# Clustered attention ahead of two expert stages: four re-ordered steps in the attention's slot schedule

## The chip, the cores and the metric

One core of one Trainium2 chip runs the whole program in one launch. The metric is the device time of the launch in microseconds (us), the median over the runs. Engines are named as the profile names them: PE is TensorE's matmul, PEld its weight load, DVE is VectorE, ACT is ScalarE, POOL is GpSimd, SP is SyncE, which here only issues DMAs. A "q" behind an engine's name is its instruction queue.

## The reference

Attention in which a query sees only keys of its own cluster, then two feed-forward stages. Shapes: 2 batches, 8 heads, 768 positions, head size 64, 16 clusters; the feed-forward stages see 1536 tokens of width 512.

```python
q_assign = argmax(normalised(q) @ normalised(centroids).T)      # per head, 16 clusters
k_assign = argmax(normalised(k) @ normalised(centroids).T)
scores = where(q_assign[:, None] == k_assign[None, :], q @ k.T / 8, -1e9)
attn = softmax(scores)                                          # over 768 keys
x = (attn @ v).reshape(1536, 512)
x = (silu(x @ w_gate) * (x @ w_val)) @ w_out                    # 512 -> 1536 -> 512
out = sum_e p[:, e] * (relu(x @ w1[e]) @ w2[e])                 # 4 experts, 512 -> 1024 -> 512
```

All of it is in 32-bit floats. The kernel gets near that precision out of faster matmuls by splitting operands in a high and a low part ("hi" and "lo", `xh` and `xl`, `wuh` and `wul`), so a product is two or three matmuls.

## The kernel before

`attention()` runs first, then `moe()`. The order of all instructions is written by hand; each engine takes its own in program order and waits for semaphores.

The attention works on 16 heads `g` (2 batches of 8), each in two halves of 384 queries, which makes 32 units `u`, and each unit in three parts, which makes 96 slots (`slot = 3u + t`). A pair `p` of heads takes 12 slots, a head 6, a unit 3. In every slot the letters of `ORDER = "ESTLAtVMlvZB"` are run through (line 564):

- `S`: four matmuls of the scores of a row block that is 5 slots ahead (`s_mm`, L325 and L326), into one of two pairs of PSUM banks;
- `M`: VectorE's row minimum or maximum over those 768 scores (`s_max`, L331); `E`: ScalarE's exponential of the block before (`s_exp`, L342), which frees the scores' bank;
- `T` and `t`: three transposes each of the exponentials (`transp`, L348), with ScalarE's copy `hi` out of PSUM (L353);
- `l` and `L`: VectorE's `lo = ps - hi` (`low`, L367), `l` for the first of the slot's two key blocks, `L`, one slot later, for the second. For the last key block of a unit `low` is a plain copy `pT` (L361);
- `V` and `v`: the products with v for the two key blocks of the slot before (`pv`, L378, L383, L384), accumulated over a unit into the tile `pv`, of which there is one PSUM bank only (`bufs=1`, line 185). So the first product of a unit (`V` in the slot with t = 1) cannot start before the bank of the unit before has been copied out;
- `A`, `Z`, `B`: extra tasks hung on a slot by `at(slot, pos, fn)` and `steps(base, when, generator)`; `("-13a", "2z")` means the generator's next step 13 slots before base at `A`, then 2 slots after it at `Z`.

The copy out of the bank is `pv_out` (lines 386 to 407). It is called at `v` in the slot with t = 0 right behind the unit's last product (`v_step`, line 587). For the pairs 0 to 6 (28 units) it is one ScalarE copy (L395), for the last pair a ScalarE copy and a VectorE add (L406, L407). Behind the fourth unit of a pair three SP DMAs move halves of `x` between partitions (L400 to L402).

The extra tasks that the change touches:

- `recip(p)` (line 409): VectorE sums and inverts the row sums of a pair, PE transposes them (L416), ScalarE copies them out, SP writes them to DRAM (`rd`, L421) and in the same step issues two DMAs (L424) that read them back, spread over 64 partitions each, as `R`. SP waits at L424 until `rd` has landed. `norm(p, G)` uses `R` at slot 9 of the pair behind, on GpSimd.
- `cluster(g)` (line 244): 12 matmuls against the centroids (L259), then the choice of the cluster. From g = 3 on it runs GpSimd `sc - mx` (L282), ScalarE `sc * HUGE` (L284), GpSimd `sc + wtie` (L286), VectorE's maximum (L288), GpSimd's subtraction (L290), ScalarE's step function (L292), 6 transposes (L296), and ScalarE writes the mask rows `mk` (L305), which two SP DMAs bring into the head's operand `t` (`t<-mk`, L307). The 12 matmuls stand 13 slots ahead of a head, the mask's DMAs 9 slots ahead; the first score matmul of that head stands 5 slots ahead of it.
- `w_steps` (line 103): the first chunk of feed-forward weights comes as 64-bit floats and is converted in 4 pieces of 512 columns. A piece is 5 steps: two ScalarE conversions with VectorE's sign mask (L113, L114, L115) and the SP load of a later piece (`w_load`, L89); VectorE's clamp (L118); shift and or (L120); add (L122); ScalarE's high part with VectorE's low part (L125, L126). Lines 556 to 561 hang these on slots 0 to 7 of every pair from p = 1 on.
- `load_v(g)` (line 229): two SP DMAs and a GpSimd DMA, 8 slots ahead of a head; `rest_v` on GpSimd (L240) 4 slots ahead. `load_qk` and `rest_qk` (L219, L220, L226) load a head's q and k on GpSimd's queue and compute their low parts on GpSimd.

`moe()` begins when the last unit is out: its matmuls (L164, L761, L858, L891) follow each other on PE with no slot schedule.

Of the kernel before, what the change touches and what calls it, by code (L numbers as in the profile page):

```python
# [7 lines left out]
F32 = mybir.dt.float32  # L8
# [4 lines left out]
ACTF = mybir.ActivationFunctionType  # L13
# [23 lines left out]
def tile_cluster_attention_moe(ctx, tc, qk, vt, cent, consts, wm1, wm2, probs, out):  # L37
# [64 lines left out]

    def w_steps(k, part, o):

        if k[0] == 1:
# [6 lines left out]
            ai = a.bitcast(I32)  # L112
            A.activation(out=a, in_=w1.bitcast(F32), func=ACTF.Abs, scale=2.0 ** -112)  # L113
            A.activation(out=ri, in_=w0.bitcast(U32), func=ACTF.Copy, scale=2.0 ** -29)  # L114
            V.tensor_scalar(out=mi, in0=w1, scalar1=-2**31, scalar2=None, op0=ALU.bitwise_and)  # L115
# [8 lines left out]
            wh, wl = w_tile(k, part, o)  # L124
            A.copy(out=wh[:, s], in_=a)  # L125
            V.tensor_tensor(out=wl[:, s], in0=a, in1=wh[:, s].bitcast(F32), op=ALU.subtract)  # L126
            yield
# [47 lines left out]
    def attention():  # L175
        with ExitStack() as ax:
# [67 lines left out]
            def cluster(g):  # L244
# [36 lines left out]
                else:  # L281
                    G.tensor_tensor(out=sc, in0=sc, in1=mx.to_broadcast([128, N, NCL]), op=ALU.subtract)  # L282
                    yield
                    A.activation(out=sc, in_=sc, func=ACTF.Copy, scale=HUGE)  # L284
                    yield
                    G.tensor_tensor(out=sc, in0=sc, in1=wb, op=ALU.add)  # L286
# [99 lines left out]
            def pv_out(u):  # L386
# [5 lines left out]
                if p < P - 1:  # L392
                    if u % 4 == 2:
                        xu_t[p].append(xp.tile([128, S], F32, tag="x1", name="x1"))
                    A.copy(out=xu_t[p][h][:, sl], in_=ps)  # L395
                    if u % 4 == 3:
                        x0, x1 = xu_t[p]
                        x2 = xp.tile([128, S], F32, tag="x2", name="x2")
                        xu_t[p] = [x0, x2]
                        SY.dma_start(out=x2[0:64], in_=x0[64:128])  # L400
                        SY.dma_start(out=x2[64:128], in_=x1[0:64])
                        SY.dma_start(out=x0[64:128], in_=x1[64:128])  # L402
                else:
                    xu = xu_t[p][0]
                    r, o = slice(64 * h, 64 * h + 64), slice(64 - 64 * h, 128 - 64 * h)
                    A.copy(out=xu[r, sl], in_=ps[o])  # L406
                    V.tensor_tensor(out=xu[r, sl], in0=ps[r], in1=xu[r, sl], op=ALU.add)  # L407

            def recip(p):
# [10 lines left out]
                rd = dram.tile([2 * NQ, 128], F32, tag="rd", name="rd")  # L420
                SY.dma_start(out=rd, in_=rT)  # L421
                R = r_t[p] = xp.tile([128, S], F32, tag="R", name="R")
                for h in range(2):
# [43 lines left out]
            for h in range(2):  # L467
                V.memset(oh_t[h], 0.0)
            V.memset(zero1, 0.0)
            mkc = clp.tile([64, 2], F32, name="mkc")  # L470
            for j, v in enumerate((1.0, 0.0, BIG, -BIG)):
# [57 lines left out]
            for i in range(4):  # L529
                at(NS - 3 + i // 2, "az"[i % 2], lambda i=i: early_up(0, i // 2, range(i % 2 * 2, i % 2 * 2 + 2)))  # L530
            steps(NS, ("-5z", "-4a", "-4z"), recip(P - 1))
            for p in range(P - 1):
                steps(12 * (p + 1), ("1a", "2z", "2b"), recip(p))
                steps(12 * (p + 1), ("8b", "9z", "10a", "10z", "11z"), norm(p, G))
            CL = ("-13a", "-13a", "-13a", "-13z", "-12z", "-12b", "-11a", "-11a", "-10a", "-10a", "-9a", "-9b", "-9b")
            CL1 = ("2a", "2z", "3a", "3a", "3z", "4a", "4z", "5a", "5z")
            CL2 = ("-12b", "-12b", "-11a", "-11a", "-11b", "-10a", "-10b", "-9a", "-9b", "-9b")
            steps(-6, CL1, head)
            for g in range(NH):
# [7 lines left out]
                if g:  # L547
                    at(c - 8, "z", lambda g=g: load_v(g))
                at(c - 4, "z", lambda g=g: rest_v(g))

            def first_weights():
                for x in pieces:
                    if x[:2] == (chunks[0], "u"):
                        yield from w_steps(*x[:3])

            weights = first_weights()
            WL = ("0b", "1a", "1z", "2b", "3a", "4a", "4z")
            WA, WB = ("0b", "2b", "7a", "7z"), ("2z", "7b", "7b")
            for p in range(1, P - 1):
                steps(12 * p, WA if p % 2 else WB, weights)  # L560
            steps(12 * (P - 1), WL, weights)

            LEAD = 5
            ORDER = "ESTLAtVMlvZB"
            for _ in range(2):
                at(9, "z", w_load)
            prev = None
            for slot in range(-LEAD, NS):
# [17 lines left out]

                def v_step():
                    pv(*prev[1])
                    if t == 0:
                        pv_out(u - 1)  # L590
# [3 lines left out]
                    "A": lambda: run(slot, "a"), "B": lambda: run(slot, "b"), "Z": lambda: run(slot, "z"),  # L594
                    "L": lambda: prev and low(*prev[1]),
                    "T": lambda: ready and transp(*cur[0]), "l": lambda: ready and low(*cur[0]),
                    "V": lambda: prev and pv(*prev[0]),
                    "t": lambda: ready and transp(*cur[1]), "v": lambda: prev and v_step(),
                }
# [358 lines left out]
```

## Time and profile before

| what | value |
|---|---|
| median of 3 runs | 1082.35 us (lowest 1081.43, highest 2118.78) |
| the profiled execution's own time | 1080.52 us |
| its span, first to last instruction | 1078.7 us |
| PE, DVE, ACT, POOL busy over the span | 98%, 64%, 43%, 18% |
| attention, from the profile's lines | about the first 290 us |

The median stands 1.8 us above the profiled execution. A "busy" matmul is one whose modelled span covers the time; PE is in order, so its real progress in the attention is better read from the starts of a line that comes six times a slot (the transposes, L348). "Idle before" in brackets is the time that an engine did nothing ahead of an instruction, with what ended it. Instructions of one engine overlap a little, so what one costs its engine is the distance from its start to the next start.

### The profile page before, as it was taken

Reading aid. Unit: us, or ns where it says so; the run is one execution under the profiler, and the core shown is the slowest. Engines: PE = TensorE matmul, PEld = TensorE weight load, DVE = VectorE, ACT = ScalarE, POOL = GpSimd, SP = SyncE. Lnnn points to the kernel's source line nnn. Section 1 sums busy time; section 2 is a strip of 40 time slices with the busy share of each in tenths; the row PEclk is TensorE's granted clock in tenths of the full one; section 3 lists DMA queues with packets and bytes.
Section 4 is the critical chain, followed back from the end, with each engine's and each line's share of the span. In section 5 each row is a group of like instructions: output and inputs, shape, how many; then the busy total and the mean of one; then the engine's idle time right before and its main releaser. Section 6 shows DMA issues by size and latency. Waiting matters only on the chain.

```text
span 1078.7 us, 13854 instructions
## 1 busy us (share of the span) xinstructions
PE 1053.4 (98%) x5189; PEld 868.9 (81%) x5189; DVE 694.2 (64%) x1211; ACT 459.0 (43%) x923; POOL 197.5 (18%) x216
## 2 busy tenths in 40 slices
PE   8899999899999999999999999999999999999998
PEld 5777877787788888888888888888888888888887
DVE  7678878778566555646748556655555656555564
ACT  6577887788544234314425222233322222333121
POOL 4347665564000000000101111111001111100100
PEclk8899999999999999999999999999999999999999
DMA  7577677642122111211201010111101011110103
GB/s 179 150 166 164 173 160 167 159 113 54 36 78 78 59 59 58 86 52 59 87 11 40 20 34 26 39 40 39 39 20 40 20 39 39 39 40 22 38 1 117
DMA packets 35332, 76.69 MB, mean 71 GB/s; under 512 B 12800, under 2 KB 17376, under 8 KB 35264
## 3 DMA queue, kind: packets, MB, share of 16 engines
q1 hardware_dynamic: 23616, 58.28, 18.3%
q0 software_dynamic: 11360, 17.44, 7.7%
q8 instruction: 41, 0.67, 0.3%
q14 instruction: 27, 0.22, 0.1%
q10 hardware_dynamic: 288, 0.07, 0.0%
HBM read 66.98 MB, written 3.19 MB: 65 GB/s over the span
## 4 chain that ended last, share of the span: by engine, by line
PE 89%; DMA 3%; ACT 3%; DVE 2%; issue 2%; POOL 1%; SPq 0%; ACTq 0%; POOLq 0%; DVEq 0%
PE pd L891 24%; PE pb L164 17%; PE pa L761 12%; PE pd L858 9%; PE pa L164 9%; PE ps L348 4%; PE ps L325 3%; PE ps L326 2%; PE pb L761 2%; PE pv L378 2%; PE pc L259 1%; PE pv L384 1%; PE pv L383 1%; DMA t<-mk 1%; PE pu L164 1%
## 5 line engine op out<-in xcount | busy, mean ns | idle before, releaser
L898 DVE SCALAR_TENSOR_TENSOR acc<-pd,pn,acc 128x512 f32<-128x512 f32 (+1 forms) x181 | 133.9, 747 | 89.5 <-PE pd L891 89.4
L891 PE MATMUL pd<-wdl,hh 128*128 128x512 f32 (+1 forms) x386 | 149.7, 388 | 0.0
L891 PE MATMUL pd<-wdh,hl 128*128 128x512 f32 (+1 forms) x386 | 149.7, 388 | 0.0
L891 PE MATMUL pd<-wdh,hh 128*128 128x512 f32 (+1 forms) x386 | 149.7, 388 | 0.0
L769 ACT COPY snap<-pa 128x512 f32<-128x512 f32 x48 | 28.2, 588 | 265.2 <-PE pa L761 265.2
L135 POOL TENSOR_TENSOR ws<-wraw 128x256 f32<-128x256 f32 x16 | 12.3, 770 | 664.3 <-DMA wraw<-in_wm 450.0
L331 DVE CUSTOM_DVE_ANT_0 junk<-ps,zero 128x768 bf16<-128x768 f32 x96 | 91.1, 949 | 21.3 <-PE ps L326 20.5
L164 PE MATMUL pb<-xh,wuh 128*128 128x512 f32 x264 | 102.7, 389 | 0.0
L164 PE MATMUL pb<-xl,wuh 128*128 128x512 f32 x264 | 102.7, 389 | 0.0
L164 PE MATMUL pb<-xh,wul 128*128 128x512 f32 x264 | 102.7, 389 | 0.0
L342 ACT ACTIVATE P<-ps,nm 128x768 f32<-128x768 f32 x96 | 87.0, 906 | 14.1 <-DVE nm L331 9.7
L348 PE MATMUL ps<-ident,P 128*128 128x128 f32 x576 | 83.9, 277 | 1.5 <-DVE lo L367 1.4
L891 PEld LDWEIGHTS pd<-wdh,hl 128*128 128x128 f32 x386 | 72.5, 188 | 15.0
L891 PEld LDWEIGHTS pd<-wdl,hh 128*128 128x128 f32 x386 | 72.5, 188 | 14.9
L891 PEld LDWEIGHTS pd<-wdh,hh 128*128 128x128 f32 x386 | 72.5, 188 | 14.9
L325 PE MATMUL ps<-t 80*128 80x512 f32 x192 | 72.0, 375 | 11.1 <-DMA t<-mk 8.5
L367 DVE TENSOR_TENSOR lo<-ps,hi 128x384 fp32r<-128x384 f32 x128 | 69.0, 553 | 15.0 <-ACT hi L353 13.6
L353 ACT CAST hi<-ps 128x384 fp32r<-128x384 f32 x128 | 58.2, 479 | 28.6 <-PE ps L348 28.6
L348 PEld LDWEIGHTS ps<-ident,P 128*128 128x128 f32 x576 | 66.7, 143 | 3.4 <-DVE lo L367 2.0
L326 PE MATMUL ps<-t 128*128 128x512 f32 x192 | 62.9, 348 | 0.0
L325 PEld LDWEIGHTS ps<-t 80*128 80x128 f32 x192 | 37.2, 194 | 31.1 <-issue 9.0
L774 ACT ACTIVATE hh<-sg 128x512 fp32r<-128x512 f32 x48 | 30.3, 632 | 72.3 <-DVE sg L781 72.3
(179 smaller groups left out, 2329.0 us busy)
## 6 DMA issues: line engine op xcount, KB each, us to landing
wraw<-in_wm SPq DMA_DIRECT2D x68, 512.0 KB, 3.6
t<-in_qk POOLq DMA_DIRECT2D x13, 768.0 KB, 5.8
raw<-in_qk SPq DMA_DIRECT2D x26, 192.0 KB, 5.2
t<-in_qk POOLq DMA_DIRECT2D x13, 384.0 KB, 6.9
x<-x SPq DMA_DIRECT2D x21, 192.0 KB, 2.8
R<-rd SPq DMA_DIRECT2D x16, 192.0 KB, 3.3
out<-acc SPq DMA_DIRECT2D x11, 256.0 KB, 2.5
rawqk<-in_qk SPq DMA_DIRECT2D x6, 384.0 KB, 3.7
```

Source lines behind the costliest of these rows:

```text
L164: T.matmul(out=ps, lhsT=w[:, o:o + 128], rhs=x, start=(k == 0 and m == 0), stop=(k == 3 and m == 2))
L325: T.matmul(out=ps, lhsT=t2[:, 0, qs], rhs=t2[:, 1, ks], start=True, stop=False)
L326: T.matmul(out=ps, lhsT=t1[:, 0, qs], rhs=t1[:, 1, ks], start=False, stop=True)
L331: V.tensor_tensor_reduce(out=junk, in0=S_t[n], in1=zero1.to_broadcast([128, S]), scale=-0.125, scalar=3.0e38, op0=ALU.add, op1=ALU.min, ac ...
L342: A.activation(out=P_t[n], in_=S_t.pop(n), func=ACTF.Exp, scale=0.125, bias=nm_t.pop(n), accum_out=rs_t[p][:, h, c:c + 1])
L348: T.transpose(ps[:, i * 128:(i + 1) * 128], P_t[3 * u + i][:, j * 128:(j + 1) * 128], ident)
L353: A.copy(out=hi, in_=ps)
L367: V.tensor_tensor(out=lo, in0=ps, in1=hi.bitcast(F32), op=ALU.subtract)
L761: T.matmul(out=ps, lhsT=w[:, o:o + 128], rhs=r, start=first and i == 0 and m == 0, stop=i == 1 and m == 2, skip_group_check=not first)
L858: T.matmul(out=ps, lhsT=w[:, o:o + 128], rhs=x[:, f, sl], start=(n == 0), stop=(n == len(terms) - 1))
L891: T.matmul(out=ps, lhsT=x[:, f, ts_], rhs=w[:, f * DM + cs.start:f * DM + cs.stop], start=(f == 0 and m == 0), stop=(f == FC - 1 and m == 2))
L898: V.scalar_tensor_tensor(out=y, in0=ps, scalar=pe, in1=y, op0=ALU.mult, op1=ALU.add)
```

## The change

- `recip` yields between the DMA that writes `rd` and the two that read it back; the broadcast is issued at slot 5 (`A`) of the pair behind, not at slot 2 (`B`).
- In `cluster`, for g from 3 on, the multiplication by HUGE moves to GpSimd (with a one-column tile `huge`, broadcast), between the two GpSimd instructions that surrounded it; the three are issued in one step, and the two slots' entries fall out of `CL`.
- `pv_out` copies with VectorE for the pairs 0 to 6, and is called at `L` in the slot with t = 1, behind that slot's `low`, not at `v` in the slot with t = 0. The last pair's two instructions move with it.
- The first chunk's weight steps are split finer (7 a piece) and hung on slots 11, 17 and 29 of every 24 for the pieces 1 to 3 (single entries for the fourth between slots 81 and 90), in place of slots 0 to 7 of each pair. The first two loads go out at slot 5, not 9.
- `load_v(1)` goes from slot -2 to slot 0.

```diff
@@ w_steps(k, part, o, fine=False)
             A.activation(out=a, in_=w1.bitcast(F32), func=ACTF.Abs, scale=2.0 ** -112)
+            if fine:
+                yield
             A.activation(out=ri, in_=w0.bitcast(U32), func=ACTF.Copy, scale=2.0 ** -29)
...
             A.copy(out=wh[:, s], in_=a)
+            if fine:
+                yield
             V.tensor_tensor(out=wl[:, s], in0=a, in1=wh[:, s].bitcast(F32), op=ALU.subtract)
@@ cluster
                     G.tensor_tensor(out=sc, in0=sc, in1=mx.to_broadcast([128, N, NCL]), op=ALU.subtract)
-                    yield
-                    A.activation(out=sc, in_=sc, func=ACTF.Copy, scale=HUGE)
-                    yield
+                    G.tensor_tensor(out=sc, in0=sc, in1=huge.rearrange("p (o c) -> p o c", o=1).to_broadcast([128, N, NCL]), op=ALU.mult)
                     G.tensor_tensor(out=sc, in0=sc, in1=wb, op=ALU.add)
@@ pv_out
-                    A.copy(out=xu_t[p][h][:, sl], in_=ps)
+                    V.tensor_copy(out=xu_t[p][h][:, sl], in_=ps)
@@ recip
                 SY.dma_start(out=rd, in_=rT)
+                yield
@@ attention
-            steps(NS, ("-5z", "-4a", "-4z"), recip(P - 1))
+            steps(NS, ("-5z", "-4a", "-4z", "-4z"), recip(P - 1))
-                steps(12 * (p + 1), ("1a", "2z", "2b"), recip(p))
+                steps(12 * (p + 1), ("1a", "2z", "2b", "5a"), recip(p))
-            CL = ("-13a", "-13a", "-13a", "-13z", "-12z", "-12b", "-11a", "-11a", "-10a", "-10a", "-9a", "-9b", "-9b")
+            CL = ("-13a", "-13a", "-13a", "-13z", "-12z", "-12b", "-10a", "-10a", "-9a", "-9b", "-9b")
-                    at(c - 8, "z", lambda g=g: load_v(g))
+                    at(0 if g == 1 else c - 8, "z", lambda g=g: load_v(g))
-                        yield from w_steps(*x[:3])
+                        yield from w_steps(*x[:3], fine=True)
-            WL = ("0b", "1a", "1z", "2b", "3a", "4a", "4z")
-            WA, WB = ("0b", "2b", "7a", "7z"), ("2z", "7b", "7b")
-            for p in range(1, P - 1):
-                steps(12 * p, WA if p % 2 else WB, weights)
-            steps(12 * (P - 1), WL, weights)
+            WS = ("-6z", "0a", "0z", "0b", "12a", "12z", "12b")
+            for i in range(3):
+                steps(17 + 24 * i, WS, weights)
+            steps(81, ("0a", "2a", "3a", "5a", "6a", "8a", "9a"), weights)
-                at(9, "z", w_load)
+                at(5, "z", w_load)
-                def v_step():
-                    pv(*prev[1])
-                    if t == 0:
+                def l_step():
+                    low(*prev[1])
+                    if t == 1 and u:
                         pv_out(u - 1)
```

## Rows read from the trace of the kernel before

**Rows 1.** Busy time by stretch: us, then each engine's busy time, granted clock, DMA.
```profile
25.00:300.00 275.00, 257.31 (x1666) 213.37 (x1664) 210.21 (x442) 207.24 (x478) 138.79 (x138) 0.98 0.57 132
300.00:1079.00 779.00, 775.41 (x3427) 642.13 (x3425) 464.73 (x719) 235.10 (x416) 48.22 (x64) 1.00 0.14 46
```

**Rows 2.** PE's timeline: first transposes of slots 6, 12 and 78 (start, us).
```profile
46.54 0.82 PE L348 MATMUL ps<-ident,P 128*128 128x128 f32 x6
...
61.20 0.82 PE L348 MATMUL ps<-ident,P 128*128 128x128 f32 x6
...
242.13 0.38 PE L348 MATMUL ps<-ident,P 128*128 128x128 f32 x2
```

**Rows 3.** PE's groups by line, from 46.5 to 242.12 us: busy, mean ns | idle before.
```profile
L348 PE MATMUL ps<-ident,P 128*128 128x128 f32 x432 | 62.6, 276 | 1.5 <-DVE lo L367 1.4
L325 PE MATMUL ps<-t 80*128 80x256 f32 (+1 forms) x145 | 53.2, 367 | 4.8 <-DMA t<-mk 4.1 <-ACT P L342 0.4
...
L378 PE MATMUL pv<-pT,vn 128*64 128x384 f32 x48 | 20.6, 512 | 3.7 <-DVE pT L361 3.7
```

**Rows 4.** Timelines of DVE and POOL around 68 us (slots 14 and 15).
```profile
68.05 2.95 DVE L118 TENSOR_SCALAR wa<-wa 128x512 f32<-128x512 f32 x1
...
68.89 1.81 POOL L226 TENSOR_TENSOR t<-raw,t 64x768 fp32r<-64x768 f32 x1
```

**Rows 5.** VectorE's weight steps by line, attention only: ns min/median/max, first and last start.
```profile
L118 DVE TENSOR_SCALAR wa<-wa x4: 428/1765/2949, 68.0 to 210.7; 128x512 f32<-128x512 f32 x4
...
L120 DVE SCALAR_TENSOR_TENSOR wa<-wa,wb x4: 701/888/928, 81.2 to 215.4; 128x512 int32<-128x512 int32 x4
...
L126 DVE TENSOR_TENSOR wul<-wa,wuh x4: 692/694/2885, 101.1 to 246.7; 128x512 fp32r<-128x512 f32 x4
```

**Rows 6.** Timelines of SP and, last, ACT around 203 us (slots 62 to 66).
```profile
198.96 0.32 SPq L421 DMA_DIRECT2D rd<-rT  x1
204.91 1.09 SPq L424 DMA_DIRECT2D R<-rd  x2
...
206.73 1.66 SPq L307 DMA_DIRECT2D t<-mk  x2
...
202.23 0.99 ACT L305 ACTIVATE mk<-pt,mkc 64x768 f32<-64x768 bf16 x1
```

**Rows 7.** The mask's DMAs by line (L307): from issue to landing.
```profile
DMA to landing us min/median/max: 2.1/3.0/5.3
```

**Rows 8.** Busy time by stretch behind the longest mask wait, columns as in the first group.
```profile
214.00:217.00 3.00, 3.00 (x14) 2.86 (x13) 2.76 (x6) 2.02 (x5) 1.59 (x3) 0.59 0.08 14
```

**Rows 9.** Copies out of a 128x384 PSUM tile, by line: ns min/median/max.
```profile
L395 ACT COPY x<-pv x28: 463/480/501, 39.9 to 258.3; 128x384 f32<-128x384 f32 x28
...
L361 DVE COPY pT<-ps x32: 543/548/559, 38.4 to 284.8; 128x384 f32<-128x384 f32 x32
```

**Rows 10.** Who waited for whom, whole program: us in total, times, longest.
```profile
POOL sc L286 <- ACT sc L284: 21.9, 13, 4.2
...
PE ps L325 <- DMA t<-mk: 8.5, 4, 4.4
```

**Rows 11.** Timelines at two beginnings of a unit (slots 78/79 and 29/30).
```profile
243.96 0.55 DVE L367 TENSOR_TENSOR lo<-ps,hi 128x384 fp32r<-128x384 f32 x1
...
245.07 0.42 PE L383 MATMUL pv<-hi,vs 128*128 128x384 f32 x1
...
110.76 0.36 DVE L268 TENSOR_TENSOR sc<-pc,sc 128x192 f32<-128x192 f32 x1 [0.83 <-ACT sc L266]
...
112.09 0.96 DVE L331 CUSTOM_DVE_ANT_0 junk<-ps,zero 128x768 bf16<-128x768 f32 x1 [0.51 <-PE ps L326]
```

**Rows 12.** POOL's timeline at the start of slot 17 (75.5 us).
```profile
74.90 1.82 POOL L226 TENSOR_TENSOR t<-raw,t 64x768 fp32r<-64x768 f32 x1 [3.46 <-DMA t<-in_qk]
```

**Rows 13.** Timelines in slot 88, the last pair's first copied bank: ACT and PE.
```profile
266.24 0.85 ACT L353 CAST hi<-ps 128x384 fp32r<-128x384 f32 x2
...
266.12 0.42 PE L383 MATMUL pv<-hi,vs 128*128 128x384 f32 x1
```

More of the change, by code (lines that the diff above doesn't have):

```diff
@@ L101, in w_tile, with w_steps @@
         return wt[k, part]
-    def w_steps(k, part, o):
+    def w_steps(k, part, o, fine=False):
         if k[0] == 1:
@@ L469, in attention @@
             V.memset(zero1, 0.0)
+            huge = clp.tile([128, 1], F32, name="huge")
+            V.memset(huge, HUGE)
             mkc = clp.tile([64, 2], F32, name="mkc")
@@ L594, in attention @@
                     "A": lambda: run(slot, "a"), "B": lambda: run(slot, "b"), "Z": lambda: run(slot, "z"),
-                    "L": lambda: prev and low(*prev[1]),
+                    "L": lambda: prev and l_step(),
                     "T": lambda: ready and transp(*cur[0]), "l": lambda: ready and low(*cur[0]),
                     "V": lambda: prev and pv(*prev[0]),
-                    "t": lambda: ready and transp(*cur[1]), "v": lambda: prev and v_step(),
+                    "t": lambda: ready and transp(*cur[1]), "v": lambda: prev and pv(*prev[1]),
                 }
```

## The prediction

> **What bounds the kernel now.** I read the busy time by stretch first. From 300 us to the end PE is busy 775 of 779 us [rows 1]: the feed-forward stages are bound by matmuls, and nothing in the change touches them. From 25 to 300 us PE, DVE and ACT all have gaps (257, 210 and 207 of 275 us): the whole effect must come out of the attention. There a "busy" matmul is no measure, so I went to PE's timeline and took the starts of the transposes, six in each slot.
>
> From 46.54 to 61.20 us PE does six slots in 14.66 us [rows 2], and the timeline shows no wait of note in them: one set of cluster matmuls, one of mask transposes, two units. I take 14.66 us as PE's own pace. From 46.54 to 242.13 us there are 432 transposes [rows 3], so 72 slots, in 195.59 us. Twelve times 14.66 is 175.92. So **19.7 us** of this stretch are stalls of PE, and that is all the steady part can give. By the groups of PE's lines they begin in two ways: 4.1 us waiting for the mask's DMA (`t<-mk`) and 3.7 us waiting for the copy `pT`, with small waits for `lo` besides [rows 3].
>
> *The mask's share.* SP issues `rd` at 198.96, and R's read-back only at 204.91, when `rd` has landed; the mask's DMA stands behind it and goes out at 206.73 [rows 6]. Its source `mk` was written by ACT from 202.23 to 203.22 [rows 6], so it lost 3.5 us in the queue. Behind that wait PE also ran 3 us at a mean granted clock of 0.59 [rows 8], between its two levels of 1.2 and 2.4 GHz, after it had stood idle: 3 x 0.41 = 1.2 us of work lost. I put 1.5 us for the whole dip, whose edges lie outside that stretch. Share: 4.1 + 1.5 = **5.6 us**.
>
> *The weight steps' share.* At 68.05 DVE's clamp L118 takes 2.95 us, and at its end GpSimd's L226, begun at 68.89 for 1.81 us, has just ended [rows 4]. The same clamp takes 0.43 us elsewhere, and L126 takes 0.69 or 2.89 us [rows 5]. So a VectorE instruction on SBUF operands that meets a run of GpSimd instructions stands still until these end, and the scores' maximum, `lo` and `pT` queue behind it. Three such stalls and the ScalarE-to-VectorE waits of the bunched steps carry what is left: 19.7 - 5.6, less 0.9 for the six transposes of reciprocals that come on top of the clean pace and stay (62.6 / 432 = 0.145 us each [rows 3]), **13.2 us**.
>
> **The change part by part.**
>
> *Broadcast of the reciprocals at slot 5.* Its two DMAs and their wait move, on SP, past the mask's two DMAs (slot 3) and `load_v`'s two (slot 4). Then the mask goes out when ACT has written it, some 3.4 us earlier in [rows 6]. Three waits make up the 4.1 us (the fourth of [rows 10], 4.4 us, is the one at the start), 1.4 on average, so 3.4 covers them unless one is far longer than the others. Behind the broadcast on SP now stand a weight load and `load_qk`'s two of slot 7, with slots to spare; its reader, GpSimd's product at slot 9, has about four slots. Gain 5.6; the bounds are 0 and 5.6.
>
> *Weight steps in slots 11, 17, 29 of 24.* These are cluster slots, where DVE idles 0.83 us ahead of the cluster's add and 0.51 us ahead of the next maximum [rows 11], and where GpSimd is mostly done. The 13.2 us go. What comes: in a slot 17, sign mask and clamp (0.43 us each, if the mask is like the clamp when that is free) and L120 (0.7 to 0.9) [rows 5], some 1.7 us against 1.3 of idle time that is not all usable, because the add waits for ACT anyway. Placed one behind the other, the next unit's bank copy then ends about 0.5 us late. In a slot 29, L122 and L126 (0.69 us for L126; I take L122, which reads as much, the same) are 1.4 us, about 0.25 us late. Three of each: 2.25 us. And GpSimd isn't always done: L226 starts at 74.90 and runs into slot 17 [rows 12], because it waits for its data. If half of the six slots meet it for about 0.7 us, that is 2.0 us; between 0 and, if all meet a whole L226, 6 x 1.8 - 6 x 0.5 of cover = 7.8. The fourth piece, slots 81 to 90: 0.4 us. The two first loads, four slots earlier on SP, pass only `load_qk`'s two and cost nothing that I can see.
>
> *Bank copy by VectorE.* ACT loses 28 x 0.480 us, DVE gains 28 x 0.548 [rows 9]. ACT's part is worth nothing by itself where PE keeps its pace. DVE's part decides: the copy now stands between the slot's second `lo` and the maximum, and the unit's first product waits for it. In a clean unit `lo` ends at 244.51, so the copy ends at 245.06, a little earlier where neighbours overlap; the product starts at 245.07 [rows 11]. The margin is next to nothing, and positive. Cost 0; the bounds are 0 and 28 x 0.55 = 15.4 (a whole copy on the path each time). Queued behind the copy on DVE are the slot's maximum and the next `lo`, up to 0.5 us later; the exponential and the product that read them come a slot later. For the last pair ACT's copy now comes behind `hi` in the slot with t = 1: `hi` runs from about 266.0, the copy to 266.9, the add to 267.4, where the product went at 266.12 [rows 13]. That is 1.3 us there, 0.4 in the next unit (which waits already), 0.1 in the last: 1.8 us.
> The Trainium skill (VectorE: DVE Perf Modes, Specifications) places VectorE nearer to SBUF and ScalarE nearer to PSUM, which speaks against this move; the trace agrees with 0.548 against 0.480 us. By that rule alone 28 x 0.07 = 2.0 us would be lost; by the margin above nothing is.
>
> *Scaling on GpSimd.* 13 ScalarE instructions go, 13 of GpSimd's come (an estimate from L226's 1.81 us for 768 columns [rows 4]: 0.45 us for 192), in a chain in which GpSimd idled 21.9 us in 13 waits for ACT [rows 10]. The chain gets shorter and nothing waits for its end. 0; the bounds are a gain of 1 us (masks a little sooner) and a loss of 6 x 0.45 = 2.7 (each weight slot meets one).
>
> *`load_v(1)`.* Three DMAs, one of them GpSimd's, move past the first mask's two DMAs on SP. These wait for ACT, not for the queue. 0, bounds 0 and the 4.4 us of the first mask wait [rows 10].
>
> **Sum.** 5.6 + 13.2 - 2.25 - 2.0 - 0.4 - 1.8 = 12.35 us less than the profiled execution's 1080.52 (a span of 1078.7 and 1.8 around it): 1068.2. The median shown stands 1.8 us above that execution, so on its scale **1070.0 us**. Own range 1064 to 1076.
>
> **Rivals.**
>
> 1. *The mask is late for another reason*: its DMA lands in 2.1 to 5.3 us [rows 7], so traffic matters. Then the broadcast's move gives nothing: 1070.0 + 5.6 = 1075.6. For it: the first mask wait, 4.4 us, is one with no read-back ahead of it. Against it: the 3.5 us lost in [rows 6]. Beside this stands the Trainium skill (DMA: Bandwidth & Descriptors, Queues, rings and completion order): a DMA engine takes turns between the queues it has work for, packet by packet; by that GpSimd's loads would slow the mask wherever SP puts it. No row here shows single packets.
> 2. *VectorE is stopped by GpSimd in the new slots too.* The six slots cost 7.8 and not 2.0 us: 1075.8; with the first rival as well, 1081.4, no change. For it: [rows 12], and once slots 14 to 16 lose their stalls, slot 17 comes sooner while L226's data don't. Against it: the chain ahead of L226 on GpSimd loses its waits for ACT [rows 10], so its loads go out sooner too.
> 3. *Slower: the single PSUM bank.* If the copy ends late in every unit, PE waits 28 times, and the maximum behind it is late as well. With 0.55 us for the copy and half of that for what it pushes, 28 x 0.83 = 23 us against 12.35 gained: 1093. It decides from 12.35 / 28 = 0.44 us a unit. For it: in-order DVE, one bank, no margin. Against it: DVE is busy 210 of 275 us [rows 1]; with 15.4 more in some 262 us it is at 86%, so it catches up within a slot or two.
> 4. *The start goes as well.* Fewer transfers before the first mask: its 4.4 us and the low clock behind it, some 6 us: 1064. Little speaks for it, since the loads that compete there are issued after it.
>
> **How the numbers follow.** Forecast 0.60, mask 0.12, GpSimd 0.12, slower 0.08, start 0.08. The range of 8 in 10 reaches from the start's case to the two middle ones with their spread: 1063 to 1080. Faster by over 2% (about what a measurement of this kernel can tell from no change) is below 1060.7: it would take all stalls and the start, 0.04. Slower by over 2% is above 1104: the third rival at (22 + 12) / 28 = 1.2 us a unit, 0.02. Within 2%: 0.94.
>
> **What would show it.** Right: the mask's wait of PE falls from 8.5 us to about 4.4; L118 and L126 have no instruction above 1 us in the attention; the 72 slots take some 181 us; the copy out of `pv` is VectorE's with 0.55 us and PE's first product of a unit waits under 0.1 us for it; the granted clock has no dip at 214. Wrong: L383 waiting 0.4 us or more behind the copy, L115, L118 or L122 of 1.5 us beside L226 in slots 17 and 29, `t<-mk` waits that stay, or R late at GpSimd's product.

## The result, and the profile after

| | before | after |
|---|---|---|
| median | 1083.48 us of 4 runs | 1072.06 us of 4 runs |
| lowest and highest | 1081.43 and 2118.78 | 1071.46 and 1072.77 |
| profiled execution, its span | 1080.52, 1078.7 | 1071.67, 1069.9 |

The ratio is 0.9901, with a 95% interval of 0.9880 to 0.9922: about 1% faster, inside the two per cent that count as no change. The forecast was 1070.0 us. One run of the kernel before took 2118.78 us; it counts in the median of the table but not in the ratio, and the other three runs have a median of 1082.35 us.

Lines of the kernel after stand 2 to 4 higher: the transposes are L350, the scores L327 and L328, the products with v L380, L385 and L386, `low` L369, the bank copy L397, the masks' DMAs L309, GpSimd's low part of a head L230.

Busy time by stretch of the kernel after, columns as in [rows 1] (us, PE, PEld, DVE, ACT, POOL, clock, DMA share, GB/s):

```profile
25.00:291.00 266.00, 257.41 (x1680) 215.15 (x1679) 218.89 (x473) 198.24 (x440) 145.37 (x151) 0.99 0.60 138
291.00:1069.00 778.00, 775.73 (x3429) 642.37 (x3427) 465.05 (x719) 235.13 (x416) 48.25 (x64) 1.00 0.14 46
...
50.00:290.00 240.00, 235.93 (x1552) 196.57 (x1551) 202.87 (x439) 184.38 (x410) 139.22 (x145) 1.00 0.62 141
```

The feed-forward stages are as they were (775.7 of 778 us busy). From 50 to 290 us the mean granted clock is 1.00, so the dip of [rows 8] (0.59 for 3 us) is gone with the wait ahead of it. ACT lost 9 us of work, DVE gained 8.7.

PE's timeline of the kernel after, first transposes of slots 0, 6 and 78 (start, us):

```profile
27.26 0.82 PE L350 MATMUL ps<-ident,P 128*128 128x128 f32 x6
...
50.22 0.82 PE L350 MATMUL ps<-ident,P 128*128 128x128 f32 x6
...
231.25 0.82 PE L350 MATMUL ps<-ident,P 128*128 128x128 f32 x6
```

The 72 slots from 50.22 to 231.25 take 181.03 us, where [rows 2] gave 195.59: 14.56 us gained. From slot 78 to the first transpose of slot 95 it is 44.05 us against 41.85: 2.2 lost. From slot 0 to slot 6 it is 22.96 against 21.70: 1.26 lost. And slot 0 itself begins 2.4 us later, 27.26 against this row of the timeline of before:

```profile
24.85 0.82 PE L348 MATMUL ps<-ident,P 128*128 128x128 f32 x6
```

14.56 - 2.2 - 1.26 - 2.4 = 8.7 us; the spans differ by 8.8. Against 1082.35 us the medians differ by 10.3. The last term belongs to one execution: in the twelve kernels below, several of which are the kernel of before up to this point, slot 0 began at 26.3 to 28.9.

PE's groups from slot 6 to slot 78 after (busy, mean ns | idle before), which answer to [rows 3]:

```profile
L327 PE MATMUL ps<-t 80*128 80x256 f32 (+1 forms) x145 | 52.3, 361 | 0.0
...
L380 PE MATMUL pv<-pT,vn 128*64 128x384 f32 x48 | 20.6, 512 | 0.1
```

The waits for the masks (4.1 us) and for `pT` (3.7) have gone to 0.0 and 0.1. Over the whole program PE's waits are now these (us in total, times, longest):

```profile
PE ps L327 <- DMA t<-mk: 4.2, 1, 4.2
PE pv L385 <- issue: 1.9, 4, 1.5
PE pv L385 <- DVE x L409: 1.4, 1, 1.4
```

One mask wait of 4.2 us is left, the one at the start; 1.4 us is the last pair's add. What is left in the 72 slots, 181.03 - 175.92 = 5.1 us, can be placed by taking each slot's length less the shortest of its kind (2.06 to 3.38 us by its place in the head). I call that a slot's excess. It adds up to 5.7 us, because the shortest slots make 175.3 in place of 175.92. The main parts are:

- 0.39 to 0.41 us in the slots 19, 31, 43, 55 and 67, together 2.0. These are the first slots with t = 1 behind a slot that holds weight steps;
- 0.92, 0.91 and 0.33 us in the slots 42, 54 and 30, together 2.2;
- 0.2 us in each of six slots that hold the reciprocals' transposes, together 1.3.

Timelines of the kernel after: a weight step in slot 41 with GpSimd beside it, then the bank copy and the product that waits for it in slot 19:

```profile
136.84 1.90 DVE L117 TENSOR_SCALAR wb<-wraw 128x512 int32<-128x512 int32 x1
...
136.66 1.81 POOL L230 TENSOR_TENSOR t<-raw,t 64x768 fp32r<-64x768 f32 x1 [2.41 <-DMA raw<-in_qk]
...
82.44 0.55 DVE L397 COPY x<-pv 128x384 f32<-128x384 f32 x1
...
83.09 0.41 PE L385 MATMUL pv<-hi,vs 128*128 128x384 f32 x1 [0.15 <-issue]
```

L117 takes 0.42 us elsewhere and 1.90 here: it ends 0.3 us after GpSimd's L230. In slot 19 the copy ends at 82.99 and the product starts 0.1 us later; PE stood idle ahead of it because DVE came late out of slot 17's weight steps.

### The profile page after: what moved, and what is told of

Same layout as the page of the kernel before. It is cut to its first block, busy times and chain, and to the rows that moved or that the text cites. A ratio compares the mean times of both kernels' runs of the same rounds, so it can differ in the third digit from the quotient of the medians.

```text
span 1069.9 us, 13863 instructions
## 1 busy us (share of the span) xinstructions
PE 1054.3 (99%) x5189; PEld 871.5 (81%) x5189; DVE 703.9 (66%) x1240; ACT 448.1 (42%) x882; POOL 203.9 (19%) x229
## 4 chain that ended last, share of the span: by engine, by line
PE 94%; DVE 2%; DMA 2%; ACT 1%; issue 1%; POOL 0%; SPq 0%; ACTq 0%; POOLq 0%; DVEq 0%
PE pd L895 24%; PE pb L168 17%; PE pa L765 12%; PE pd L862 9%; PE pa L168 9%; PE ps L350 5%; PE ps L327 3%; PE ps L328 3%; PE pv L380 2%; PE pb L765 2%; PE pv L385 2%; PE pv L386 2%; PE pc L263 1%; PE pu L168 1%; DMA x<-x 1%
## 5 line engine op out<-in xcount | busy, mean ns | idle before, releaser
L344 ACT ACTIVATE P<-ps,nm 128x768 f32<-128x768 f32 x96 | 86.6, 902 | 20.6 <-DVE nm L333 19.7
L350 PE MATMUL ps<-ident,P 128*128 128x128 f32 x576 | 83.5, 276 | 0.1
L327 PE MATMUL ps<-t 80*128 80x512 f32 x192 | 72.4, 377 | 5.4 <-DMA t<-mk 4.2
L369 DVE TENSOR_TENSOR lo<-ps,hi 128x384 fp32r<-128x384 f32 x128 | 68.4, 552 | 10.2 <-ACT hi L355 9.1
L350 PEld LDWEIGHTS ps<-ident,P 128*128 128x128 f32 x576 | 66.0, 142 | 2.5 <-issue 0.6
L328 PE MATMUL ps<-t 128*128 128x512 f32 x192 | 63.5, 351 | 0.0
L168 PEld LDWEIGHTS pb<-xl,wuh 128*128 128x128 f32 x264 | 49.6, 188 | 10.3
```

The source lines that it names most:

```text
L168: T.matmul(out=ps, lhsT=w[:, o:o + 128], rhs=x, start=(k == 0 and m == 0), stop=(k == 3 and m == 2))
L327: T.matmul(out=ps, lhsT=t2[:, 0, qs], rhs=t2[:, 1, ks], start=True, stop=False)
L328: T.matmul(out=ps, lhsT=t1[:, 0, qs], rhs=t1[:, 1, ks], start=False, stop=True)
L344: A.activation(out=P_t[n], in_=S_t.pop(n), func=ACTF.Exp, scale=0.125, bias=nm_t.pop(n), accum_out=rs_t[p][:, h, c:c + 1])
L350: T.transpose(ps[:, i * 128:(i + 1) * 128], P_t[3 * u + i][:, j * 128:(j + 1) * 128], ident)
L369: V.tensor_tensor(out=lo, in0=ps, in1=hi.bitcast(F32), op=ALU.subtract)
```

## The experiments

Below, "the mask's waits" are PE's waits for `t<-mk`. Every ratio stands beside runs of the kernel before, with medians of 1083.7 to 1084.6 us. Times by stretch and the excess come from one profiled execution of each kernel; single executions of the kernel before lay between 1080.2 and 1087.3 us, so a difference of 1 or 2 us between two profiles is shown only where a median or a named wait bears it out. The edits carry the diff's own lines.

**One part alone: the broadcast at slot 5.**

```diff
                 SY.dma_start(out=rd, in_=rT)
+                yield
...
-                steps(12 * (p + 1), ("1a", "2z", "2b"), recip(p))
+                steps(12 * (p + 1), ("1a", "2z", "2b", "5a"), recip(p))
```

> The kernel before with the broadcast's later place alone. Theory (the masks stand behind the read-back on SP): three of the four waits of PE for the masks go, 4.1 us, with the clock's dip 5.6 us: 1077.9 against 1083.5. Rival (traffic sets the masks' landing): waits stay near 8.5 us and the time at 1083.

Measured: 1078.14 us, ratio 0.9945 [0.9933, 0.9957]. The 72 slots take 190.07 us, 5.5 less. PE's wait for the masks, in this kernel:

```profile
PE ps L325 <- DMA t<-mk: 3.8, 1, 3.8
```

Only the wait at the start is left. The mask of the head in [rows 6], in SP's timeline of this kernel:

```profile
203.89 1.19 SPq L307 DMA_DIRECT2D t<-mk  x2
```

ACT has written it at 203.87, so it goes out at once, where the kernel before lost 3.5 us. So the masks of the steady part were late because the read-back stood ahead of them on SP (L424). The masks' DMAs also land sooner, in 2.2 us in the median against 3.0 [rows 7]; whether the read-back's own transfer slowed them, no run separates.

**One part alone: the weight steps.** The diff's hunks in `w_steps`, `first_weights`, `WS` and `w_load`, on the kernel before.

```diff
-            WA, WB = ("0b", "2b", "7a", "7z"), ("2z", "7b", "7b")
+            WS = ("-6z", "0a", "0z", "0b", "12a", "12z", "12b")
+            for i in range(3):
+                steps(17 + 24 * i, WS, weights)
```

> The kernel before with the weight steps' new places alone (and the loads at slot 5). Theory: 13.2 us of stalls go, 3 to 4 us come back in the new slots, so 1073 to 1075; without the bank copy on VectorE the slots behind a weight slot (19, 43, 55) should show less than the 0.4 us they have in the changed kernel. Rival (the stalls move with the steps): above 1079.

Measured: 1071.23 us, 0.9887 [0.9865, 0.9909]; its six runs lie between 1068.3 and 1075.3. The 72 slots take 183.58 us, 12.0 less, and more than expected. The excess of 0.4 us in the slots 19, 31, 43, 55 and 67 is not there. The mask's waits stay, 8.0 us in four.

**Both of these and nothing else.**

> The kernel before with the broadcast's later place and the weight steps' new places, without the other three parts. Theory (the two gains act on different waits and add): 1083.6 - 5.5 - 12.5 = 1065.6, faster than the changed kernel by 6 us. Rival (the parts are worth only together, the room on ScalarE among them): 1070 or more.

Measured: 1065.49 us, 0.9835 [0.9815, 0.9855]: 6.6 us faster than the whole change. The 72 slots take 177.51 us, 1.6 above PE's own pace, of which the reciprocals' transposes are 0.7. PE's scores from slot 6 to slot 78 in this kernel (no wait for a mask):

```profile
L329 PE MATMUL ps<-t 80*128 80x256 f32 (+1 forms) x145 | 52.7, 363 | 0.0
```

So the other three parts together cost the change its 6.6 us. By stretches, after against this kernel: 22.96 to 21.29 in the slots 0 to 6, 181.03 to 177.51 in the 72, 44.05 to 42.24 in the tail, 7.0 us in all.

**One part alone: the bank copy.**

```diff
-                    A.copy(out=xu_t[p][h][:, sl], in_=ps)
+                    V.tensor_copy(out=xu_t[p][h][:, sl], in_=ps)
...
-                    if t == 0:
+                    if t == 1 and u:
                         pv_out(u - 1)
```

> The kernel before with the bank copy's move alone (VectorE, slot with t = 1, the last pair's two instructions too). Theory (a unit's copy is hidden in a clean slot, costs 0.4 us behind a slot that loads VectorE and 2 us in the last pair, and what it spares ScalarE is worth nothing): 3 to 6 us slower than before, 1086 to 1090. Rival (ScalarE's waits for the unit's last product hold PE, so it pays): at or below 1083.

Measured: 1097.98 us, 1.0135 [1.0113, 1.0156]. That is 13.4 us slower and far outside what I expected. PE's mask waits, SP's waits for `rd`, and the stretch behind the longest mask wait (columns as in [rows 1]), in this kernel:

```profile
PE ps L325 <- DMA t<-mk: 19.8, 6, 6.2
```

```profile
SPq L424 <- DMA rd<-rT: 37.0, 8, 8.1
```

```profile
88.90:92.00 3.10, 3.10 (x12) 2.91 (x13) 1.20 (x3) 0.75 (x3) 0.00 (x0) 0.50 0.29 88
```

The mask waits grow by 11.3 us (8.5 before), and behind the longest of them the granted clock is 0.50. SP's timeline around the broadcast of the first pair, in this kernel and then, one line, in the kernel before:

```profile
66.95 0.33 SPq L89 DMA_DIRECT2D wraw<-in_wm  x1
67.33 0.52 SPq L400 DMA_DIRECT2D x<-x  x1
67.90 0.59 SPq L401 DMA_DIRECT2D x<-x  x1
73.84 0.46 SPq L402 DMA_DIRECT2D x<-x  x1
...
75.67 0.55 SPq L421 DMA_DIRECT2D rd<-rT  x1
83.39 1.10 SPq L424 DMA_DIRECT2D R<-rd  x2
84.55 1.22 SPq L307 DMA_DIRECT2D t<-mk  x2
```

```profile
58.44 0.52 SPq L400 DMA_DIRECT2D x<-x  x1
```

The cost seems to sit mostly in SP's order and not at the bank. Called a slot later, the three `x` DMAs of this pair stand behind a weight load (L89); in the kernel before, the first of them (L400) went out 6 us ahead of that load. The third (L402) then waits 5.3 us until the first has landed; `rd` goes out only behind it, the read-back stands 7.7 us behind `rd`, and the mask behind that, 8.7 us after ACT has written it (4.0 before). In the other pairs `rd` goes out as soon as its data are there, but SP waits longer at L424 for it to land: 37.0 us in all against 31.5 before. Why it lands later, no run shows. If SP's order is the cause, the copy costs little where the broadcast stands at slot 5.

**Bank copy and broadcast together.** Both diffs above on the kernel before.

> The kernel before with the bank copy's move and the broadcast's later place, no other part. Theory A (alone, the bank copy's later place holds SP at the pair's x DMAs, and these push rd, its read-back and the masks behind them; with the read-back out of the way that loss goes): the bank copy costs here 3 to 5 us on top of the broadcast alone (1078.1), 1081 to 1083, and the masks' waits are about 4 us. Theory B (the copy on VectorE itself costs the 13 us that it cost alone): 1091.

Measured: 1080.66 us, 0.9963 [0.9950, 0.9976]: 2.5 us over the broadcast alone, where the bank copy alone cost 13.4. SP's timeline at the same place:

```profile
74.22 0.55 SPq L421 DMA_DIRECT2D rd<-rT  x1
74.86 1.20 SPq L307 DMA_DIRECT2D t<-mk  x2
```

The mask goes out 0.6 us behind `rd`, and its waits are 4.9 us in two. With the read-back out of the way the copy's price falls by 11 us, so that much of it was SP's chain. What is left is the last pair's: the 72 slots take 189.76 us (190.07 with the broadcast alone), slots 78 to 95 take 44.15 (41.84). Without the new weight steps, VectorE's copies of the other pairs cost nothing.

**One part alone: the scaling on GpSimd.** The diff's hunk in `cluster`, its tile `huge` and `CL`.

```diff
-                    yield
-                    A.activation(out=sc, in_=sc, func=ACTF.Copy, scale=HUGE)
-                    yield
+                    G.tensor_tensor(out=sc, in0=sc, in1=huge..., op=ALU.mult)
```

> The kernel before with the scaling on GpSimd alone. Theory (nothing waits for the chain's end, and GpSimd's longer runs may hold VectorE's weight steps a little): within 1 us of before, 1083.6. Rival (ScalarE's 13 instructions were on the path in the loaded slots): 2 us or more faster.

Measured: 1084.78 us, 0.9998 [0.9981, 1.0015]: nothing, in twelve runs. GpSimd's three instructions take 0.5 us each.

**The change with ScalarE's bank copy at its old place.**

```diff
-                    V.tensor_copy(out=xu_t[p][h][:, sl], in_=ps)
+                    A.copy(out=xu_t[p][h][:, sl], in_=ps)
...
-                    if t == 1 and u:
+                    if t == 0:
                         pv_out(u - 1)
```

> The changed kernel with ScalarE copying the bank again, in the slot with t = 0, for all pairs; the rest kept. Theory: the 0.4 us of the slots 19, 31, 43, 55 and 67, the 0.35 of slot 85 and the tail's 2 us go: about 5 us faster than 1072.1, 1067. Rival (ScalarE's copy brings back as much as it spares): 1071 to 1073.

Measured: 1067.2 us, 0.9849 [0.9829, 0.9869]: some 5 us faster than the change, of which the last pair is 2.1 (next experiment). The excess in the slots 19, 31, 43, 55, 67 and 85 is 0.0 here. In the 72 slots it also was 0.0 with the bank copy and the broadcast but without the new weight slots. So it needs both: weight steps make DVE late in one slot, and the bank copy in the next stands behind them. VectorE's stalls beside GpSimd stay: not in the slots 42, 54 and 30, but in 18 and 66, with 1.6 and 1.3 us of excess, behind an L120 of 1.94 and one of 1.68 us beside L230 (0.42 alone). The 72 slots take 179.68 us, 2.2 more than with the two useful parts alone; the scaling on GpSimd and `load_v(1)` are all that lies between these two kernels.

**The change with only the last pair's copy at its old place.**

```diff
-                    if t == 1 and u:
+                    if t == 1 and 0 < u <= NS // 3 - 4:
                         pv_out(u - 1)
+                def v_step():
+                    pv(*prev[1])
+                    if t == 0 and u > NS // 3 - 4:
+                        pv_out(u - 1)
```

> The changed kernel with the last pair's copy out of the bank back in the slot with t = 0, the other 28 copies kept on VectorE in the slot with t = 1. Theory (the ScalarE copy and VectorE add behind hi hold the unit's first product): slot 88 takes 2.1 us instead of 3.8, the kernel is about 2 us faster than 1072.1: 1070. Rival (the tail is set by the chain of the last transposes and the place costs nothing in the end): the time from slot 84 to the last slot stays at 30.0 us, 1072.

Measured: 1069.97 us, 0.9871 [0.9855, 0.9888]. Slot 88's excess goes from 1.71 to 0, slot 91's from 1.06 to 0.02, and slots 78 to 95 take 41.72 us instead of 44.05. This is what it removes, in the timelines of ACT, DVE and PE in slot 88 of the kernel after:

```profile
255.15 0.48 ACT L355 CAST hi<-ps 128x384 fp32r<-128x384 f32 x1 [0.33 <-PE ps L350]
255.66 0.48 ACT L408 COPY x<-pv 64x384 f32<-64x384 f32 x1
...
256.22 0.55 DVE L409 TENSOR_TENSOR x<-pv,x 64x384 f32<-64x384 f32 x1 [1.49 <-POOL x L436]
...
256.82 0.45 PE L385 MATMUL pv<-hi,vs 128*128 128x384 f32 x1 [1.44 <-DVE x L409]
```

`hi`, copy, add, product: one behind the other, 1.44 us of idle PE.

**The change with `load_v(1)` back at slot -2.**

```diff
-                    at(0 if g == 1 else c - 8, "z", lambda g=g: load_v(g))
+                    at(c - 8, "z", lambda g=g: load_v(g))
```

> The changed kernel with load_v(1) back at slot -2, all else kept. Theory A (the move costs the start): the first transposes of slot 6 come at about 46.5 us again instead of 50.2, the clustering's VectorE step in slot 2 has no 2 us instance, and the kernel is 3 to 4 us faster than the changed one's 1072.1: about 1068.5. Theory B (the start differs by the phase in which VectorE's casts and GpSimd's low parts meet around 15 us, whatever load_v does): only the 1.2 us of slots 2 and 3 come back, slot 6 begins at about 49 us, 1071.

Measured: 1071.83 us, 0.9887 [0.9872, 0.9903], not to be told from the change. Slot 0 begins at 27.57, so this part is not what moved it. But slot 3's excess goes from 0.90 to 0. The timelines of DVE and POOL in the kernel after show why:

```profile
38.84 1.99 DVE L277 TENSOR_TENSOR eq<-sc,mx 128x192 bf16<-128x192 f32 x1
...
35.46 0.72 POOL L244 TENSOR_TENSOR vs<-vraw,vs 128x256 fp32r<-128x256 f32 x1 [6.68 <-DMA vraw<-in_vt]
36.15 1.81 POOL L230 TENSOR_TENSOR t<-raw,t 64x768 fp32r<-64x768 f32 x1
...
38.78 1.84 POOL L230 TENSOR_TENSOR t<-raw,t 64x768 fp32r<-64x768 f32 x1
```

GpSimd's L244 waits 6.68 us for the later load, so its second low part comes to stand beside the second head's cluster steps, and L277 takes 1.99 us; with the load early it takes 0.35. That depends on when the two meet: the two kernels above that keep the late load have 1.3 us of excess in slot 3, and the next one has none. The time does not follow because the 72 slots are 1.6 us longer in that profile (slots 18 and 66, 1.3 and 1.0 of excess).

**Where is GpSimd's low part free of VectorE?** In the change, that of even heads one slot later.

```diff
-("-19b", "-15a") if g % 2 else ("-19b", "-15b")
+("-19b", "-15a") if g % 2 else ("-18b", "-15b")
```

> The changed kernel with GpSimd's first low part of the even heads (the one that meets the weight steps of slots 17, 29, 41, 53) one slot later, behind the cluster's GpSimd instructions of slot 6. Theory (VectorE's weight steps stand still behind it in some of the slots): no weight step over 1.1 us, the 0.9 us of slots 42 and 54 go, 1070 to 1071 against 1072.1. Rival (it holds something else as long): 1072 or more.

Measured: 1078.61 us, 0.9953 [0.9936, 0.9970], slower than the change by 6 us; the rival was right. The excess of the slots 42 and 54 did go, from 0.92 and 0.91 to 0.06 and 0.00. But PE has a new wait, here in the profile of the slowest of its ten runs:

```profile
PE pc L263 <- POOL t L230: 6.2, 5, 1.3
```

and from the timelines of DVE (one line) and POOL:

```profile
149.59 0.34 DVE L290 TENSOR_REDUCE mx<-sc 128x12 f32<-128x192 f32 x1
...
148.89 1.83 POOL L230 TENSOR_TENSOR t<-raw,t 64x768 fp32r<-64x768 f32 x1
...
153.02 1.82 POOL L436 TENSOR_TENSOR x<-x,x 128x768 f32<-128x768 f32 x1
154.92 1.84 POOL L441 TENSOR_TENSOR x<-x,R 128x768 f32<-128x768 f32 x1
156.72 1.81 POOL L230 TENSOR_TENSOR t<-raw,t 64x768 fp32r<-64x768 f32 x1
```

The next low part falls behind the two products of `norm`, and the cluster matmuls of its head wait for it. The low part has a reader on PE with no slack of a slot.

**The first mask.** The kernel with the two useful parts, and GpSimd's loads of head 4 held back until the first mask has landed. ACT writes one column `gate` in slot 1, behind the products that wait for the mask; GpSimd overwrites it and so waits.

```diff
+                    if g == 4:
+                        at(1, "a", lambda: A.copy(out=gate, in_=zero1))
+                        at(1, "z", lambda: G.memset(gate, 0.0))
                     at(c - 23, "z", lambda g=g: load_qk(g))
```

> The broadcast-and-weights kernel (1065.5) with GpSimd's loads of head 4 held back until ScalarE has finished a slot-1 instruction that comes behind the first mask's arrival. Theory A (these 1.1 MB, issued within a microsecond of the first mask's DMAs, are why the mask lands in 5.7 us and not in the usual 3.0): PE's wait at the start falls from 4.0 to about 1.5 us, the low clock behind it shortens, 1062 to 1063. Theory B (the mask's DMA is slow there for another reason): the wait stays at 4 us, 1065.5.

Measured: 1065.46 us, 0.9824 [0.9808, 0.9840], no change against the two useful parts alone. The DMA issues from 20 to 40 us (KB each, median us to landing), first with the two useful parts alone, then with the gate:

```profile
t<-in_qk POOLq DMA_DIRECT2D x1, 768.0 KB, 5.2
t<-in_qk POOLq DMA_DIRECT2D x1, 384.0 KB, 6.6
...
t<-mk SPq DMA_DIRECT2D x2, 48.0 KB, 5.4
```

```profile
t<-mk SPq DMA_DIRECT2D x2, 48.0 KB, 2.6
```

Beside 1.1 MB of GpSimd's loads, issued 0.5 and 1.0 us behind it, the mask lands in 5.4 us, without them in 2.6. PE's wait for it falls from 4.0 to 1.2 us and slot 0's excess from 5.1 to 1.7. The gain is gone again by slot 24. Timelines of DVE and POOL with the gate:

```profile
35.67 1.79 DVE L278 TENSOR_TENSOR eq<-eq,wtie 128x192 bf16<-128x192 bf16 x1
...
38.99 1.67 DVE L282 TENSOR_TENSOR oh<-eq,mw 128x192 bf16<-128x192 bf16 x1
```

```profile
35.39 1.95 POOL L230 TENSOR_TENSOR t<-raw,t 64x768 fp32r<-64x768 f32 x1
...
38.65 1.80 POOL L230 TENSOR_TENSOR t<-raw,t 64x768 fp32r<-64x768 f32 x1 [0.57 <-issue]
```

The gate holds back all that stands behind it on GpSimd, its low parts too, and these now meet cluster steps of 0.26 and 0.35 us, which take 1.79 and 1.67 (2.1 us of excess in slot 3, 1.6 in slot 18).

**The first mask, with GpSimd's work ahead of the gate.** The gate and `load_qk(4)` at slot 3, so that GpSimd does L244 and a low part before it.

```diff
-                        at(1, "z", lambda: G.memset(gate, 0.0))
-                    at(c - 23, "z", lambda g=g: load_qk(g))
+                        at(3, "z", lambda: G.memset(gate, 0.0))
+                    at(3 if g == 4 else c - 23, "z", lambda g=g: load_qk(g))
```

> This is e10 with the rest of the loads re-ordered: the loads of heads 1 and 3 go out before the first mask, and only the loads of head 4 wait behind it, issued in slot 3. Theory (slot 0 keeps the 3.5 us that e10 won there, and the 2.1 us that e10 gave back in slot 3 go, because GpSimd's low parts then run outside VectorE's cluster steps): about 1063 us. Rival (the start has no slack to give: GpSimd's low parts only move to other cluster steps of the first slots, and slot 18's weight step still meets one): 1065.5 us, as e8 and e10.

Measured: 1062.78 us, 0.9810 [0.9787, 0.9832], the fastest of all: 9.3 us under the change. Timelines of POOL and DVE in this kernel:

```profile
20.90 1.80 POOL L230 TENSOR_TENSOR t<-raw,t 64x768 fp32r<-64x768 f32 x1
...
38.72 1.82 POOL L230 TENSOR_TENSOR t<-raw,t 64x768 fp32r<-64x768 f32 x1 [3.36 <-issue]
```

```profile
37.37 0.35 DVE L282 TENSOR_TENSOR oh<-eq,mw 128x192 bf16<-128x192 bf16 x1
...
38.51 1.02 DVE L371 TENSOR_TENSOR lo<-ps,hi 128x384 fp32r<-128x384 f32 x2
```

One low part runs at 20.90, ahead of all cluster steps, the other at 38.72, behind them. L371, with one operand in PSUM, runs beside it at its usual 0.5 us. Slot 3's excess is 0, slot 0's 1.9, and slots 0 to 6 take 18.23 us instead of 21.29.

## Why the prediction was right, and where it was not

The median came out 2.1 us above the forecast: inside the range of 8 in 10 (1063 to 1080) and inside the forecast's own (1064 to 1076).

- *PE's own pace and the 72 slots.* The step was 175.92 us of work and 19.7 us of stalls, and some 181 us after the change. It is 181.03. This step carried the rest. The terms for these slots, 5.6 + 13.2 - 2.25 - 2.0, make 14.55 us where 14.56 were measured; that they meet so closely is luck: in the profiles of the two kernels that differ from the change only outside these slots (the last pair's copy early, `load_v(1)` early) they take 182.06 and 182.67 us.
- *The mask's share, 5.6 us.* Right: alone the broadcast gives 5.5 us in the 72 slots, and the dip of the clock is gone.
- *The weight steps, 13.2 us gone.* Right: with the broadcast already moved, the new places give 190.07 - 177.51 = 12.6 us. How much of it was VectorE beside GpSimd, and how much the bunched steps, no run separates.
- *2.25 us for bank copies late behind weight steps.* Right in mechanism and size: 2.0 us in the five slots behind weight steps. It was booked to the weight steps, but it takes both parts: with ScalarE's copy, or without the weight steps, those excesses are 0.0.
- *2.0 us for VectorE beside GpSimd.* 2.2 us, in three of the six slots: L117 takes 1.90, L124 2.35 and L130 1.24 us. So two of the prediction's signs of being wrong did appear (L115, now L117, beyond 1.5 us; a product 0.4 us behind the copy), at the price that the sum had for them. With the two useful parts alone this price is 0.8 us.
- *Bank copy, 0 in clean units.* Right: with the broadcast moved and the old weight steps, the 72 slots are no longer than without it. But "cost 0" as a property of this part is wrong. On the kernel before it cost 13.4 us, by a way I had not named: the `x` DMAs come to stand elsewhere in SP's order, and `rd`, read-back and mask behind them. The change hides this only because it moves the broadcast as well.
- *Last pair, 1.8 us, and the fourth piece of weights, 0.4.* Their sum is the 2.2 us measured from slot 78 to 95, but the pair alone is 2.3 (44.05 against 41.72): 1.7 us in slot 88, with 1.44 of idle PE against 1.3, and 1.1 in slot 91 against 0.4. In slot 88 `hi` starts at 266.24 in [rows 13], not at 266.0; from there the sum gives 1.5. The fourth piece costs nothing that shows: with the weight steps alone, slots 78 to 95 take 41.60 us against 41.85.
- *Scaling, 0.* Right on the kernel before. In the change it is not shown: the scaling and `load_v(1)` together go with 1067.2 against 1065.49 us, and with 2.2 us of the 72 slots, in stalls of VectorE beside GpSimd. The intervals of these two medians overlap, and no run has the scaling alone beside the new weight slots.
- *`load_v(1)`, 0.* Wrong for the slots 0 to 6, by some 1 us. I asked only what the load passes on SP. What counted was its reader, GpSimd's L244, and what stands behind that on GpSimd. Put back, the 1 us did not show in the median.
- *The span's own offset.* The forecast went from one profiled execution, 1.8 us under the median shown. That execution began slot 0 some 1.5 to 4.1 us earlier than the thirteen other profiles. Why the first 25 us differ between executions I did not test. This and the slots 0 to 6 are where the 2.1 us of the miss lie as far as the profiles tell.

Rival 1, traffic, did not decide in the steady part and is true for the first mask: 5.4 us to land against 2.6. The Trainium skill (DMA: Bandwidth & Descriptors, Queues, rings and completion order) says that a DMA engine alternates between the queues it has work for, a packet at a time; the two landings agree with that, though no run here shows packets. Rival 2, GpSimd in the new slots, is true for 2.2 of its 7.8 us. Rival 3, the slower one, did not decide: its point was 0.44 us a unit, and the copy cost 0.4 us in 5 units of the 72 slots' 24. Alone, the same part was slower, but mostly by SP's chain, not at the bank. Rival 4 did not come; it took a gate for it.

## What to carry to other kernels

Test each part of a bundle alone and in pairs: here two parts gave 19 us and the other three took 7 back, and the price of one of them, the bank copy with its last pair, was 13, 5 or 2.5 us depending on its neighbours. When a step is moved, follow its readers as well as the queue it moves past: a DMA that comes to stand behind another one, or the next job of an engine that waits for a load, is where the cost appears. When a held-back transfer frees one wait, see what else was held back with it before calling the wait harmless.

## What the runs showed of the hardware

VectorE's tensor-tensor and tensor-scalar instructions on SBUF operands stand still beside a GpSimd instruction, however small they are: 0.26 us became 1.79, 0.35 became 1.67 and 1.99, 0.42 became 1.90. One with an operand in PSUM ran beside the same GpSimd instruction at its usual 0.5 us. Nor does every instruction on SBUF stand still: the cluster's maximum, a reduction of one operand, took its usual 0.34 us inside L230 (149.59, in the kernel with the low part a slot later). I knew it from the large weight steps, and had not expected it of the cluster steps. The Trainium skill (SBUF — State Buffer, SBUF: two separate sides) gives the rule: VectorE and GpSimd share a pair of ports, which a VectorE instruction needs when it has two inputs in SBUF or runs in a mode that takes both ports; whichever of the two starts first holds the pair for its whole instruction, and the other waits. The trace agrees, and the reduction that ran on has one input; in which mode an instruction ran, no run here shows. The trace shows one thing more: the clamp of [rows 4] began 0.84 us ahead of GpSimd's L226, beside the GpSimd instructions in front of it, and still ended 0.3 us after L226, so it waited for more than one instruction in a row.

Where these two engines meet shifts with little. With `load_v(1)` early, the gain in slots 2 to 4 was given back in slots 18 and 66. The kernel with the low part a slot later ran between 1074.9 and 1083.4 us; that these meetings cause the spread is not shown. Whether one schedule can keep every low part clear of every such step was not tried.
